# A softmax-routed expert kernel on one core: tokens laid out by unit pairs, stores with rows of 8 KB, and new order lists

## The chip, the core and the metric

The kernel runs on 1 of the 8 cores of one Trainium2 chip, as one program. The metric is the device time of an execution, in microseconds (us). A core has five engines with a queue each: TensorE (PE, its weight loads shown apart as PEld), VectorE (DVE), ScalarE (ACT), GpSimd (POOL) and SyncE (SP, which here only issues DMAs). Sixteen DMA engines move the data of all queues.

## The reference

Two layers follow each other. The first is a gated recurrence over the time axis, for 4 sequences of 5056 tokens with 256 channels; the second is a soft mixture of 8 experts with 4 slots each, over all 20224 tokens of the first one's output:

```python
# recurrence: per channel, along the tokens of a sequence
sig_r, sig_i = sigmoid(r_gate), sigmoid(i_gate)
a_t = exp(8.0 * sig_r * log(clip(sigmoid(a_param), 1e-6, 1 - 1e-6)))
x_gated = sqrt(maximum(1 - a_t * a_t, 1e-6)) * sig_i * x
h = a_t[:, t] * h + x_gated[:, t];  y[:, t] = h
# soft mixture: X is y as (20224, 256)
logits = X @ phi                                 # (20224, 32)
d = softmax of logits over all tokens            # per slot
slot_input = d.T @ X                             # (32, 256)
slot_out[e] = relu(slot_input[e] @ w1[e]) @ w2[e]   # w1 (256, 1024), w2 (1024, 256)
c = softmax of logits over the 32 slots          # per token
out = c @ slot_out                               # (20224, 256)
```

The sum over all tokens in `d.T @ X` splits the kernel: nothing can be stored before the last token has been scanned and the experts have run.

## The kernel before, in words

Tokens are cut into 40 blocks (quads) of QT = 512, the last of 256. UNITS puts them together: block 0 alone, then pairs (1,2), (3,4) to (37,38), and block 39 alone: 21 units. Every piece of work is a task of a planner, named by kind and number, and the lists ORDER write out for each engine in which order the tasks stand in its queue. An engine takes them strictly in that order. The durations that are given to the tasks were used to find an order; with ORDER set they only decide where warm-up transposes go and which buffer a task gets.

The tasks that matter here, by name:

- D (SP) loads r, i or x of a block: partition p holds 4 tokens that follow each other, so a row of 4 KB. SP's queue ends with the stores OD.
- TR, SR: PE transposes r, ACT takes tanh of it. The result goes to A, which holds channels on partitions and the unit's tokens in time order along the row. SI is the gate of i, EX the exponential (ACT), SQ the square (POOL), RT the square root (ACT), U the product of gate and x (POOL), TU its transposes (PE), ST and SC the scaling and the scan (DVE), which leaves h in A.
- TY (PE, L958) transposes h back to tokens on partitions, four transposes for 256 tokens, and YC copies it from PSUM to the buffer yn, on DVE or ACT.
- Blocks form groups of softmax, g = 0 to 10. LG (PE, L1009) gives the logits of up to 4 blocks at once, 32 partitions for each block. LE (DVE, L1022) keeps them and takes the running maximum M; LD subtracts it (POOL, and DVE for the last two groups), TE transposes, ES takes exp (ACT), AC (PE, L1083) multiplies with yn, AE adds it into accS with the correction DM (ACT).
- For the softmax over slots of each group: CT (PE, L1438) transposes the logits, CM and CS subtract the maximum (DVE), CE takes exp (ACT, L1455), RR sums (DVE, L1459), CN scales (POOL), CH and CL split the result in a high and a low part (DVE, POOL).
- The seam: after the last scan SC20.1 come LE9, LE10, the merging of the strips' maxima (MT, MX, MR, MC, WJ, WE, W), AC9, AC10, AE10, SP and SL (the slot inputs), then L1 and L2 for the 8 experts (PE, L1331 and L1379) with HS, HT, HR between them, SO, RS, SH and BD.
- The output: HP transposes the split weights of 8 x 128 tokens, HE copies them, OT (PE, L1526, two matmuls) makes 256 tokens of output, OE copies that from PSUM (ACT L1538, DVE L1540), and OD (SP, L1550) stores a block of 512 tokens from one buffer.

Before the change A is read in time order. LG takes 512 columns that follow each other, TY 128; CT reads every 4th column, and thereby its rows come out as the store needs them, 4 tokens on each partition.

Of the kernel before, what the change touches and what calls it, by code (L numbers as in the profile page):

```python
# [76 lines left out]
SIGR = False  # L77
CG = 3
ORDER = {
    "PE": """  # L80
# [8 lines left out]
        LG7.1 TY30.0 TU18.0 TY30.2 TY31.0 TY31.2 TE7 TU18.1 TY33.0 TY33.2 AC7.0 AC7.1 AC7.2 AC7.3 TU19.0 TY34.0 TY32.2 LG8.0 LG8.1 TY34.2 TY35.0
        TY36.0 TU19.1 TY36.2 TE8 TY35.2 LG9.0 AC8.0 AC8.1 TU20.0 TU20.1 LG9.1 AC8.2 AC8.3 LG10.0 LG10.1 TY37.0 TY37.2 TY39.0 MT TY38.0 TE9 TY38.2 TE10  # L90
        MC AC9.0 AC9.1 AC9.2 AC9.3 AC10.0 AC10.1 SP DN L1.0 L1.1 L1.2 L1.3 L1.4 HT0 L1.5 L1.6 L2.0 L2.1 L1.7 L2.2 HT1 L2.3 L2.4 L2.5 L2.6 L2.7 HP0.8
        HP0.0 RS HP2.0 CT3 HP1.8 HP1.0 OT0.6 OT0.4 OT0.2 OT0.0 OT0.12 OT0.8 OT1.0 OT1.2 OT0.10 OT0.14 OT1.6 OT1.4 CT6 HP2.8 CT4 OT2.2 OT2.0 OT2.6
# [11 lines left out]
        YC29.2 RT18.0 YC30.0 YC30.2 YC31.0 DM7 ES7 RT19.0 YC33.0 YC33.2 EX20.0 YC34.0 YC32.2 SI39 CE0 YC34.2 EX20.1 YC36.0 YC35.0 YC36.2 ES8 YC35.2
        RT20.0 CE1 YC37.2 DM8 CE2 YC37.0 YC38.0 ES9 YC39.0 ES10 DM10 WE YC38.2 DM9 HE0.0 BD01 BD00 OE0.4 HE1.0 OE0.2 CE3 OE1.2 OE0.10 HE1.8 HE2.0
        OE0.14 OE1.4 OE1.6 OE2.0 OE2.2 HE2.8 CE4 OE2.12 OE2.14 OE2.8 OE1.12 HE3.8 OE2.10 CE6 OE1.10 HE3.0 OE3.8 CE5 OE3.10 OE3.12 OE3.2 HE4.0 OE3.14
        OE3.4 OE3.6 OE4.0 OE4.8 CE7 OE4.12 OE4.6 HE5.8 HE5.0 OE4.10 OE5.6 OE5.8 OE5.10 OE5.2 CE8 OE5.12 HE6.8 OE5.14 OE6.12 OE6.4 OE6.6 CE9 OE6.8
# [9 lines left out]
        YC25.2 ST14.1 ST14.0 SC14.1 SC14.0 ST15.1 YC24.2 SC15.1 ST15.0 AE5 LE6 SC15.0 YC26.0 ST16.0 SC16.0 ST16.1 YC27.2 YC28.0 SC16.1 YC28.2 ST17.0
        AE6 SC17.0 ST17.1 LE7 SC17.1 ST18.0 YC31.2 SC18.0 ST18.1 AE7 SC18.1 ST19.0 LE8 SC19.0 ST19.1 SC19.1 ST20.0 ST20.1 SC20.0 SC20.1 LE9 RR0 LE10
        LD9 LD10 MX MR WJ AE8 AE9 W AE10 CH0 SL RD HS0 HR0 RR1 HS1 HR1 CH1 RR2 CH2 SO HE0.8 SH BD11 BD10 CM3 CS3 OE0.6 OE0.0 OE0.8 OE1.0 RR3 OE0.12
        CM6 CS6 CM4 CS4 OE2.4 CH3 OE2.6 RR4 OE1.14 OE1.8 CH4 CM5 CS5 CM7 RR6 OE3.0 RR5 HE4.8 CS7 CH5 OE4.4 OE4.2 RR7 CH6 OE4.14 CM8 OE5.4 CH7 CS8  # L120
# [1468 lines left out]
```

## Time and profile before

| what | us |
|---|---|
| median of 3 runs | 300.62 (299.88 to 300.74) |
| the profiled execution | 300.04 |
| its span, from the first to the last instruction | 298.3 |
| busy PE / DVE / ACT / POOL | 259.9 / 232.3 / 251.2 / 204.5 |
| moved by DMA | 100.02 MB (78.94 MB read, 20.71 MB written) |
| mean granted TensorE clock | 0.988 |

Times inside the trace count from the span's start. In rows of the time line the columns are the start, the duration of all instructions that the row merges, the engine, the line, the operation, what it writes and reads, and how many; a bracket tells the idle time before and who ended it. A line number is one of the kernel before, and several tasks of a kind share one line.

### The profile page before, as it was taken

What the parts mean: (1) busy time and instruction counts of PE and PEld (TensorE: products, weight loads), DVE (VectorE), ACT (ScalarE), POOL (GpSimd) and SP (SyncE); (2) the same over time, 40 slices, a digit from 0 to 9 for tenths busy, and PEclk for the clock granted to TensorE, in tenths of its full rate; (3) what the DMA queues carried; (4) which work ended last, traced back from release to release, by engine and by line L of the source; (5) the groups of instructions that cost most, each with busy time, mean ns of one, the idle gap of its engine ahead of it and who ended that gap; (6) DMA issues with size and microseconds to landing.
All of it is one profiled execution on the core that took longest, in us unless ns stands there. A gap on an engine that the chain in (4) does not pass through costs nothing.

```text
span 298.3 us, 5854 instructions
## 1 busy us (share of the span) xinstructions
PE 259.9 (87%) x2223; PEld 198.9 (67%) x2223; DVE 232.3 (78%) x289; ACT 251.2 (84%) x271; POOL 204.5 (69%) x150
## 2 busy tenths in 40 slices
PE   6998698899897997969978888999989999999990
PEld 6997697577564864747656556566556588888760
DVE  0047849898979999899999999999962489896820
ACT  5899999999999999997999999999650058978680
POOL 4297999778999798997499998983431513372310
PEclk9999999999999999979999999999999999999997
DMA  6999999997875999794996499599999029999997
GB/s 229 414 409 409 402 408 410 407 408 281 322 291 208 396 415 407 274 401 116 396 392 264 174 335 365 229 385 362 358 405 351 6 78 398 404 402 404 402 409 288
DMA packets 30287, 100.02 MB, mean 335 GB/s; under 512 B 3378, under 2 KB 3380, under 8 KB 30260
## 3 DMA queue, kind: packets, MB, share of 16 engines
q1 hardware_dynamic: 30256, 99.66, 86.6%
q8 instruction: 17, 0.28, 0.4%
q14 instruction: 10, 0.08, 0.1%
q10 hardware_dynamic: 4, 0.00, 0.0%
HBM read 78.94 MB, written 20.71 MB: 334 GB/s over the span
## 4 chain that ended last, share of the span: by engine, by line
PE 35%; ACT 24%; DVE 14%; DMA 11%; POOL 6%; issue 6%; SPq 0%; ACTq 0%; POOLq 0%; DVEq 0%
DVE b L934 7%; PE bank L1526 7%; DMA b<-in_i_gate_dram 6%; PE pair L788 5%; ACT b L881 4%; DVE pair L917 4%; PE pair L900 4%; POOL b L834 4%; ACT b L812 3%; DMA st<-in_moe_w_dram 3%; ACT b L799 3%; ACT b L866 3%; PE one L1526 3%; ACT L881 3%; POOL b L850 2%
## 5 line engine op out<-in xcount | busy, mean ns | idle before, releaser
L850 POOL TENSOR_TENSOR b<-b 128x1024 f32<-128x1024 f32 (+2 forms) x41 | 73.6, 1816 | 9.0 <-ACT b L866 4.7
L834 POOL TENSOR_TENSOR b<-b,b 128x1024 f32<-128x1024 f32 x32 | 75.4, 2379 | 6.0 <-ACT b L814 4.3
L917 DVE SCALAR_TENSOR_TENSOR pair<-b,pair 128x1024 f32<-128x1024 f32 (+2 forms) x42 | 47.9, 1154 | 11.9 <-ACT b L881 8.1
L900 PE MATMUL pair<-ident,b 128*128 128x128 f32 x380 | 49.4, 278 | 7.3 <-DVE b L934 3.0
L900 PEld LDWEIGHTS pair<-ident,b 128*128 128x128 f32 x380 | 42.3, 143 | 15.7 <-POOL b L834 4.7
L934 DVE TENSOR_TENSOR_SCAN b<-b,pair 128x1024 f32<-128x1024 f32 (+6 forms) x26 | 47.6, 1848 | 0.2
L788 PE MATMUL pair<-ident,st 128*128 128x128 f32 x316 | 42.1, 280 | 5.2 <-DVE b L934 2.1
L934 DVE TENSOR_TENSOR_SCAN b<-b,b,pair 128x1024 f32<-128x1024 f32 (+2 forms) x22 | 45.4, 2073 | 0.4
L788 PEld LDWEIGHTS pair<-ident,st 128*128 128x128 f32 x316 | 35.4, 143 | 12.8 <-ACT b L799 4.9
L799 ACT ACTIVATE b<-pair 128x1024 f32<-128x1024 f32 (+1 forms) x40 | 39.4, 1012 | 4.6 <-PE pair L788 4.4
L866 ACT ACTIVATE b<-b,ca 128x2048 f32<-128x2048 f32 (+3 forms) x24 | 42.7, 1795 | 0.2
L958 PE MATMUL one<-ident,b 128*128 128x128 f32 x208 | 31.6, 281 | 7.2 <-DVE yn L974 2.5
L958 PEld LDWEIGHTS one<-ident,b 128*128 128x128 f32 x208 | 22.6, 141 | 17.3 <-DVE yn L974 6.6
L1526 PE MATMUL bank<-bd,hT 128*128 128x512 f32 x118 | 31.7, 400 | 0.3 <-DVE hT L1516 0.3
L1469 POOL TENSOR_TENSOR b<-b,rs_all 128x512 f32<-128x512 f32 (+2 forms) x11 | 10.6, 960 | 29.8 <-DVE rs_all L1461 23.2
L881 ACT ACTIVATE b<-b 128x2048 f32<-128x2048 f32 (+2 forms) x17 | 29.8, 1785 | 0.1
L1514 ACT CAST hT<-bank 128x512 fp32r<-128x512 f32 x14 | 8.3, 600 | 21.4 <-PE bank L1503 20.6
L812 ACT ACTIVATE b<-b 128x2048 f32<-128x2048 f32 x14 | 26.0, 1906 | 0.1
L1526 PEld LDWEIGHTS bank<-bd,hT 128*128 128x128 f32 x118 | 21.3, 188 | 5.4 <-ACT st L1538 0.8
L1538 ACT COPY st<-bank 128x512 f32<-128x512 f32 x33 | 18.8, 603 | 6.9 <-PE bank L1526 4.5
L974 DVE COPY yn<-one 128x512 f32<-128x512 f32 x32 | 21.2, 682 | 2.2 <-PE one L958 2.1
L1009 PE MATMUL one<-b,phi_sb 128*32 128x512 f32 x152 | 21.3, 618 | 0.0
(146 smaller groups left out, 438.4 us busy)
## 6 DMA issues: line engine op xcount, KB each, us to landing
b<-in_x_dram SPq DMA_DIRECT2D x39, 512.0 KB, 7.4
st<-in_r_gate_dram SPq DMA_DIRECT2D x38, 512.0 KB, 8.1
b<-in_i_gate_dram SPq DMA_DIRECT2D x38, 512.0 KB, 8.4
b<-in_moe_w_dram SPq DMA_DIRECT2D x28, 512.0 KB, 6.2
out_dram<-st SPq DMA_DIRECT2D x28, 512.0 KB, 4.4
out_dram<-b SPq DMA_DIRECT2D x10, 512.0 KB, 4.6
st<-in_moe_w_dram SPq DMA_DIRECT2D x4, 512.0 KB, 8.0
st<-in_r_gate_dram SPq DMA_DIRECT2D x3, 256.0 KB, 2.9
```

The source lines that it names most:

```text
L788: nc.tensor.transpose(out=o[:, m, :], in_=raw("r", q)[:, m * D + h * P : m * D + (h + 1) * P], identity=ident,)
L799: nc.scalar.activation(dst, t(rp)[:, :, :c], AF.Sigmoid if SIGR else AF.Tanh, scale=1.0 if SIGR else 0.5)
L812: nc.scalar.activation(v, v, AF.Sigmoid)
L834: eng.tensor_tensor(out=o, in0=a, in1=b, op=ALU.mult)
L850: eng.tensor_tensor(out=t(Nb[p])[:, h, :c], in0=v, in1=v, op=ALU.mult)
L866: nc.scalar.activation(v, v, AF.Exp, scale=ca[:, h : h + 1], bias=ca[:, h : h + 1])
L881: nc.scalar.activation(v, v, AF.Sqrt, bias=quarter if f != 1.0 else f, scale=-f)
L900: nc.tensor.matmul(o[:, m, :], raw(nm, q)[:, m * D + h * P : m * D + (h + 1) * P], ident, is_transpose=True, start=(nm == nms[0] and m == ...
L917: nc.vector.scalar_tensor_tensor(v, t(Nb[p])[:, h, :c], 0.5e-3 if gate_of(quads(p)[0]) == "E" else 1e-3, v, op0=ALU.max, op1=ALU.mult)
L934: nc.vector.tensor_tensor_scan(dst, dst, flat()[:, s0:s1], init, op0=ALU.mult, op1=ALU.add)
L958: nc.tensor.transpose(out=flat()[:, b * D + h * P : b * D + (h + 1) * P], in_=t(A[p])[:, h, o : o + P], identity=ident,)
L1526: nc.tensor.matmul(t(op), t(hT)[:, b * P // 2 : (b + 2) * P // 2], T["bd"][part].rearrange("p i d -> p (i d)"), start=(part == 0), stop=(p ...
```

## The change

The unit, not the block, now decides which token lies where on the way back to token order. In a pair of 1024 tokens, partition c takes tokens 8c to 8c + 7. So column m of the transposed h is every 8th column of A (every 4th in block 0, every 2nd in block 39), and `tokens` gives that view to TY and LG. From there on, the two blocks of a pair are the lower and the upper four columns m, not its first and second 512 tokens. CT then reads columns that follow each other. The output of a pair lies in one buffer of 2048 floats per partition, and one store writes it with rows of 8 KB. The first group keeps separate stores of half rows for blocks 1 and 2.

Groups follow the units: 3 blocks, nine times 4 blocks (two units each), and the last one of 256 tokens as two strips of 128. Before there were nine groups of 4, one of 2, and one of three half blocks. As group 0 fills only 96 partitions, M and accS are preset for the rest. LD of the last two groups may go to DVE or POOL (it is on DVE still). The loads of r, i, x and the weights are the same, in another order. There are 22 stores where there were 41, and 41 AC where there were 42.

The core of the diff (of ORDER, all of whose lists change, one place; of the planner's durations, which change by a few hundredths of a microsecond, two):

```diff
     "DVE": """
-        ... SC20.0 SC20.1 LE9 RR0 LE10
-        LD9 LD10 MX MR WJ AE8 AE9 W AE10 CH0 SL RD HS0 HR0 RR1 ...
+        ... SC20.0 SC20.1 LE9 LE10 AE8 LD9 LD10 YC38.2 MX MR
+        WJ W AE9 AE10 SL RR1 RR2 RR0 RD HS0 CH1 HR0 ...
...
-            lat = {"PE": 0.25, "ACT": 0.13, "DVE": 0.13, "POOL": 0.12, "SP": 2.6}[eng[0]]
+            lat = {"PE": PEL, "ACT": 0.13, "DVE": 0.13, "POOL": 0.12, "SP": 2.6}[eng[0]]
...
-    groups = [[(q, 0, QT) for q in range(g, g + J)] for g in range(0, NQ - J, J)]
-    rest = list(range(len(groups) * J, NQ))
-    groups.append([(q, 0, QT) for q in rest[:2]])
-    half = QT // 2
-    tail = []
-    for q in rest[2:]:
-        tail += [(q, o, half) for o in range(0, qlen(q), half)]
-    assert len(rest) == J and len(tail) <= J and all(qlen(q) % half == 0 for q in rest)
-    groups.append(tail)
+    groups = [[(q, 0, QT) for q in range(J - 1)]]
+    groups += [[(q, 0, QT) for q in range(g, g + J)] for g in range(J - 1, NQ - 1, J)]
+    groups.append([(NQ - 1, o, P) for o in range(0, qlen(NQ - 1), P)])
     NGR = len(groups)
+    assert sorted({q for sg in groups for q, _, _ in sg}) == list(range(NQ)) and qlen(NQ - 1) == 2 * P
+
+    def tokens(q, b0=0, nb=J):
+
+        p, i = unit[q]
+
+        def view(h):
+            v = t(A[p])[:, h, : plen(p)].rearrange("q (c m) -> q m c", c=P)
+            k = i * J + b0
+            return v[:, k, :] if nb == 1 else v[:, k : k + nb, :]
+
+        return view
     if tc is not None:
         M = sb.tile([P, NGR], F32, name="M")
         dm = sb.tile([P, NGR], F32, name="dm")
...
+        first = NS * len(groups[0])
+        nc.gpsimd.memset(M[first:, 0:1], NEG)
+        nc.gpsimd.memset(accS[first:], 0.0)
 
     t_const = add("POOL", "const", 2.1, prio=-100, emit=e_const)
...
                 for b in range(nb):
-                    o = i * QT + (b0 + b) * P
                     for h in range(H):
                         nc.tensor.transpose(
                             out=flat()[:, b * D + h * P : b * D + (h + 1) * P],
-                            in_=t(A[p])[:, h, o : o + P],
+                            in_=tokens(q, b0 + b, 1)(h),
                             identity=ident,
                         )
 
...
                 for j, (q, o, _) in enumerate(segs):
-                    o += unit[q][1] * QT
                     nc.tensor.matmul(
                         t(lp)[32 * j : 32 * j + NS, :L], phi_sb[:, h, :],
-                        t(A[unit[q][0]])[:, h, o : o + L], start=(h == 0), stop=(h == H - 1),
+                        tokens(q, o // P, L // P)(h), start=(h == 0), stop=(h == H - 1),
                     )
 
-            lg = add("PE", f"LG{g}.{h}", L * 0.00195,
+            lg = add("PE", f"LG{g}.{h}", L * 0.0019,
                      deps=[SC[(p, h2)] for p in ps_ for h2 in range(h + 1)] + [ld[("x", PHI)]], gate=begun(lg),
                      prio=pos - LGP + fin, emit=e_lg, alloc=[] if h else [lp],
...
-        deng = LDENG if g < NGR - 2 else "D"
+        both = g >= NGR - 2
+        deng = {}
 
...
         def e_ae():
             if g == 0:
-                nc.vector.tensor_copy(out=accS, in_=t(acc)[:, : D + 1])
+                nc.vector.tensor_copy(out=accS[:rows], in_=t(acc)[:rows, : D + 1])
             else:
                 nc.vector.scalar_tensor_tensor(
...
-            v = lS(g)[:rows, :L].rearrange("q (p n) -> q n p", n=nb)
+            v = lS(g)[:rows, :L].rearrange("q (n p) -> q n p", n=nb)
...
-        ogs = [Buf(("st", "b", "yn"), f"og{g}.{j}") for j in range(n)]
-        for og in ogs:
-            og.late = ("begun", l1s[-1])
+        wide = {}
+        ogs = []
+        for j, (q, o, _) in enumerate(segs):
+            p, i_ = unit[q]
+            if len(quads(p)) == 2 and i_ or o:
+                ogs.append(ogs[-1])
+            else:
+                ogs.append(Buf("b" if len(quads(p)) == 2 else ("st", "yn", "b"), f"og{g}.{j}"))
+                ogs[-1].late = ("begun", l1s[-1])
+            wide[j] = (unit[q][1] * J if o == 0 else 1) * D if len(quads(p)) == 2 or o else 0
...
-                def e_oe(b0=b0, op=op, og=ogs[j]):
-                    dst = t(og)[:, b0 * D : (b0 + 2) * D]
+                def e_oe(b0=b0, op=op, og=ogs[j], w=wide[j]):
+                    dst = t(og)[:, w + b0 * D : w + (b0 + 2) * D]
...
+        js = []
         for j, (q, o, _) in enumerate(segs):
-
-            def e_od(q=q, o=o, L=L, nb=nb, og=ogs[j]):
-                a0 = q * QT + o
-                nc.sync.dma_start(
-                    out=out[a0 : a0 + L, :].rearrange("(p n) d -> p (n d)", n=nb), in_=t(og)[:, : nb * D])
-
-            add("SP", f"OD{g}.{j}", 1.30 * nb / J, deps=done[j], prio=100 + 8 * i + 4 + j, emit=e_od, uses=[ogs[j]], kind="out")
+            if o:
+                continue
+            two = len(quads(unit[q][0])) == 2
+            if two and g > 0 and unit[q][1]:
+                continue
+            def e_od(q=q, og=ogs[j], g=g):
+                p, i = unit[q]
+                t0 = UNITS[p][0] * QT
+                v = out[t0 : t0 + plen(p), :].rearrange("(m n) d -> m (n d)", n=plen(p) // P)
+                s = t(og)[:, : plen(p) // P * D]
+                if g == 0 and len(quads(p)) == 2:
+                    v, s = v[:, i * J * D : (i + 1) * J * D], s[:, i * J * D : (i + 1) * J * D]
+                nc.sync.dma_start(out=v, in_=s)
+            of = [j] if g == 0 else [j, j + 1] if two or L < QT else [j]
+            add("SP", f"OD{g}.{j}", 1.28 * (2 * P if L < QT else QT * len(of)) / QT, deps=[x for a in of for x in done.get(a, [])],
+                prio=100 + 8 * i + 4 + j, emit=e_od, uses=[ogs[j]], kind="out")
```

How the lists move the instructions is shown at three places. Numbers behind a name are buffers. DVE from the two last scans of block 39 (L934), before:

```order
L934 SCALAR_TENSOR_TENSOR b_66<-b_66,b_69,pair_92 128x256
L934 SCALAR_TENSOR_TENSOR b_66<-b_66,b_69,pair_93 128x256
L1021 COPY M<-M 32x1 x2
L1022 TENSOR_SCALAR b_73,M<-one_86,M 64x512
L1459 TENSOR_REDUCE rs_all<-b_66 128x16
L1460 TENSOR_SCALAR rs_all<-rs_all 128x16
L1461 RECIPROCAL rs_all<-rs_all 128x16
L1021 COPY M<-M 32x1
L1022 TENSOR_SCALAR b_73,M<-bank_2111,M 96x256
L1042 TENSOR_SCALAR lD_83<-one_86,M 64x512
L1042 TENSOR_SCALAR lD_82<-bank_2111,M 96x256
```

After (L947 is the scan, L1033 is LE, L1114 AE, L1058 LD, L986 YC):

```order
L947 SCALAR_TENSOR_TENSOR b_74<-b_74,b_68,pair_92 128x256
L947 SCALAR_TENSOR_TENSOR b_74<-b_74,b_68,pair_93 128x256
L1033 TENSOR_SCALAR b_66,M<-one_86,M 128x512
L1032 COPY M<-M 32x1 x2
L1033 TENSOR_SCALAR b_66,M<-bank_2096,M 64x128
L1114 SCALAR_TENSOR_TENSOR accS<-accS,dm,one_87 128x257
L1058 TENSOR_SCALAR lD_83<-one_86,M 128x512
L1058 TENSOR_SCALAR lD_82<-bank_2096,M 64x128
L986 COPY yn_76<-bank_2098 128x2x256
L1283 TENSOR_REDUCE mmax<-bank_2101 1x32
L1285 COPY mrep<-mmax 1x128
```

The sums of group 0 (L1459 to L1461) have left the place between the two maxima; AE8 and a copy YC38.2 have come in behind them.

PE at the first output matmuls (OT, two rows each; hT is the transposed weight buffer that HE fills, bd the expert outputs), before:

```order
L1526 MATMUL bank_2112<-bd_2203,hT_2206 128x512
L1526 MATMUL bank_2112<-bd_2204,hT_2206 128x512
L1526 MATMUL bank_2116<-bd_2203,hT_2206 128x512
L1526 MATMUL bank_2116<-bd_2204,hT_2206 128x512
L1526 MATMUL one_86<-bd_2203,hT_2206 128x512
L1526 MATMUL one_86<-bd_2204,hT_2206 128x512
L1526 MATMUL bank_2111<-bd_2203,hT_2205 128x512
L1526 MATMUL bank_2111<-bd_2204,hT_2205 128x512
```

After:

```order
L1549 MATMUL bank_2096<-bd_2185,hT_2188 128x512
L1549 MATMUL bank_2096<-bd_2186,hT_2188 128x512
L1549 MATMUL bank_2101<-bd_2185,hT_2187 128x512
L1549 MATMUL bank_2101<-bd_2186,hT_2187 128x512
L1549 MATMUL bank_2099<-bd_2185,hT_2187 128x512
L1549 MATMUL bank_2099<-bd_2186,hT_2187 128x512
L1549 MATMUL bank_2098<-bd_2185,hT_2188 128x512
L1549 MATMUL bank_2098<-bd_2186,hT_2188 128x512
L1549 MATMUL bank_2100<-bd_2185,hT_2188 128x512
L1549 MATMUL bank_2100<-bd_2186,hT_2188 128x512
```

Before, OT0.6 and OT0.4, which fill block 1, stand first. Now OT0.6, OT0.8, OT0.10 and OT0.4 follow each other, and the second half of block 1 is the fourth.

SP where the last weight loads end and the stores begin, before:

```order
L1236 DMA b_69<-in_moe_w_dram 128x1024 x2
L1238 DMA b_67<-in_moe_w_dram 128x2x512 x4
L1550 DMA out_dram<-st_64 128x1024
L1550 DMA out_dram<-st_63 128x1024
L1550 DMA out_dram<-st_65 128x1024
L1550 DMA out_dram<-st_62 128x1024
L1550 DMA out_dram<-b_66 128x1024
L1550 DMA out_dram<-st_64 128x1024
```

After:

```order
L1253 DMA b_66<-in_moe_w_dram 128x2x512 x2
L1585 DMA out_dram<-b_69 128x1024
L1585 DMA out_dram<-st_64 128x1024
L1585 DMA out_dram<-b_69 128x1024
L1585 DMA out_dram<-b_75 128x2048
L1585 DMA out_dram<-b_66 128x2048
L1585 DMA out_dram<-b_73 128x2048 x2
L1585 DMA out_dram<-b_75 128x2048
```

The stores of 128 x 1024 floats become 128 x 2048 after the first three.

More of the change, by code (lines that the diff above doesn't have):

```diff
@@ L77 @@
 SIGR = False
+SIWITH = {}
 CG = 3
@@ L89 @@
[L89 to L92, printed above, removed]
@@ new lines @@
+        TY33.0 TY35.0 TY33.2 TE8 TY36.2 TY35.2 AC8.0 AC8.1 LG9.0 TU20.0 TU20.1 AC8.2 LG9.1 AC8.3 LG10.0 LG10.1 TY38.0 TY38.2 TY37.0 TY37.2 MT TE9
+        TY39.0 TE10 MC AC9.0 AC9.1 AC9.2 AC9.3 AC10.0 SP DN L1.0 L1.1 L1.2 L1.3 L1.4 HT0 L1.5 L1.6 L1.7 L2.0 CT3 HT1 L2.1 L2.2 L2.3 L2.4 L2.5 L2.6
+        L2.7 HP0.8 HP0.0 RS CT6 HP1.0 HP2.0 OT0.6 OT0.8 OT0.10 OT0.4 OT0.0 OT0.2 OT1.2 OT1.0 OT1.4 OT1.6 OT2.4 OT2.2 OT2.0 OT2.6 CT5 CT4 HP1.8 HP3.0
+        HP2.8 HP3.8 OT1.8 OT1.14 OT1.12 OT1.10 OT2.12 OT2.8 OT2.10 OT3.10 OT2.14 OT3.12 OT3.8 OT3.14 OT3.0 OT3.4 CT7 HP4.8 HP4.0 CT10 OT3.2 OT3.6
@@ L104 @@
[L104 to L107, printed above, removed]
@@ new lines @@
+        RT12.0 RT11.0 YC18.0 YC17.0 RT13.0 YC18.2 SR27 SR28 SR29 YC17.2 DM4 SR30 SR31 EX14.0 SR33 EX14.1 SR32 SR34 ES4 EX16.0 EX16.1 DM5 ES5 SI27 SI29
+        RT14.0 RT17.0 RT15.0 SI31 SI33 SR35 SR37 RT16.0 YC23.2 YC25.0 SR36 SR38 YC25.2 EX18.0 YC27.0 ES6 EX18.1 DM6 SI35 YC28.0 SR39 SI37 RT18.0
+        YC29.0 YC31.2 YC29.2 YC30.0 DM7 ES7 YC30.2 RT19.0 YC32.2 EX20.0 SI39 YC34.0 EX20.1 YC36.0 YC34.2 YC33.0 YC35.0 YC33.2 ES8 YC36.2 RT20.0 DM8
+        YC35.2 YC38.0 DM9 YC37.0 YC37.2 ES9 ES10 YC39.0 WE CE1 DM10 CE2 CE0 HS1 CE3 HE0.0 BD00 BD01 OE0.6 OE0.0 OE0.10 HE2.0 OE0.8 CE6 OE1.6 OE1.2
@@ L117 @@
[L117 to L120, printed above, removed]
@@ new lines @@
+        YC11.2 YC12.2 YC15.0 YC16.0 YC13.2 SC9.1 YC15.2 CM2 AE3 CS2 YC16.2 ST10.0 ST10.1 SC10.0 SC10.1 ST11.0 SC11.0 LE4 ST11.1 SC11.1 ST12.0 SC12.0
+        ST12.1 SC12.1 ST13.0 LE5 SC13.0 ST13.1 AE4 SC13.1 YC23.0 YC22.0 YC20.0 YC21.0 YC19.0 YC19.2 YC21.2 YC20.2 YC22.2 ST14.0 ST14.1 SC14.0 SC14.1
+        ST15.0 AE5 SC15.0 ST15.1 YC24.0 SC15.1 LE6 YC24.2 ST16.0 YC26.0 SC16.0 ST17.0 YC26.2 SC17.0 ST16.1 LE7 SC16.1 AE6 YC27.2 YC31.0 ST17.1 YC28.2
+        SC17.1 ST18.0 YC32.0 ST18.1 SC18.0 SC18.1 AE7 ST19.0 LE8 ST19.1 SC19.0 SC19.1 ST20.0 ST20.1 SC20.0 SC20.1 LE9 LE10 AE8 LD9 LD10 YC38.2 MX MR
@@ L173 @@
 class Buf:
[L176 removed]
+    __slots__ = ("tags", "tag", "slot", "users", "name", "need", "late", "mate", "kept", "led")
     def __init__(self, tags, name=""):
@@ L436, in tag_for @@
     def tag_for(self, b, taken={}):
+        if b.led and b.kept is None:
+            return None
         for g in b.tags:
@@ L1019, in e_le @@
         def e_le():
-            for r0 in range(rows, P, 32):
+            for r0 in range(rows, P, 32) if g else ():
                 nc.vector.tensor_copy(out=M[r0 : r0 + 32, g : g + 1], in_=M[r0 : r0 + 32, g - 1 : g])
@@ L1275, in merge_tasks @@
             out=small["wj"], in0=mm, in1=t(mp)[:, P : P + 1], op=ALU.subtract))
-        a = add("ACT", "WE", 0.2, deps=[a], prio=-60, kind="exp",
+        a = add("ACT", "WE", 0.1, deps=[a], prio=-60, kind="exp",
                 emit=lambda: nc.scalar.activation(small["wj"], small["wj"], AF.Exp))
@@ L1453, in mk_c @@
                     out=cn(), in0=v3(t(cp)), in1=t(rm)[:, :m, :].broadcast_to([P, m, NS]), op=ALU.subtract))
-        e = add("ACT", f"CE{g}", 0.12 + 0.43 * nb * rows / QT, deps=[k], prio=pr, kind="exp", gate=("gates_done",),
+        e = add("ACT", f"CE{g}", 0.1 + 0.43 * nb * rows / QT, deps=[k], prio=pr, kind="exp", gate=("gates_done",),
                 uses=[lSb[g // 4]], emit=lambda: nc.scalar.activation(lS(g)[:, : m * NS], lS(g)[:, : m * NS], AF.Exp))
```

128 lines of the change are left out of this document (66 added, 62 removed).

## The prediction

> **What bounds the kernel now.** I read the busy tenths first, then the sums over stretches, then what ScalarE (ACT) waited for, and last the seam between the two halves and the output, instruction by instruction. The page first, cut to ACT, the DMA engines and what they moved in 40 slices of 7.5 us:
>
> ```profile
> ACT  5899999999999999997999999999650058978680
> ...
> DMA  6999999997875999794996499599999029999997
> GB/s 229 414 409 409 402 408 410 407 408 281 322 291 208 396 415 407 274 401 116 396 392 264 174 335 365 229 385 362 358 405 351 6 78 398 404 402 404 402 409 288
> ```
>
> ACT is full until slice 28 and the DMA engines from slice 34 on; in slice 32 neither does anything. The sums (PE, PEld, DVE, ACT, POOL busy, the clock, DMA share, GB/s) and ACT's waits after 15 us (in total, times, longest):
>
> ```profile
> 15.00:212.00 197.00, 172.24 (x1524) 130.43 (x1524) 178.11 (x167) 193.72 (x166) 172.22 (x92) 0.99 0.89 342
> 227.00:230.00 3.00, 3.00 (x54) 1.74 (x49) 1.74 (x5) 0.00 (x0) 0.00 (x0) 1.00 1.04 380
> 246.00:292.00 46.00, 43.45 (x227) 35.13 (x225) 33.14 (x71) 37.20 (x73) 16.35 (x16) 1.00 1.01 403
> ...
> ACT b L799 <- PE pair L788: 2.2, 3, 1.5
> ```
>
> From 15 to 212 us ACT idles 197.00 - 193.72 = 3.3 us, so before the seam an order can win only what it takes off ACT and some of those 3.3 us. PE has 24.8 us of idle there. From 246 us the stores run at 403 GB/s with a DMA share above 1, and PE beside them is 94% busy: a co-bound.
>
> The seam, on VectorE (DVE) and then PE, from the end of the last scan:
>
> ```profile
> 213.99 0.31 DVE L1021 COPY M<-M 32x1 f32<-32x1 f32 x2
> 214.31 0.74 DVE L1022 TENSOR_SCALAR_CACHE_REDUCE b<-one,M 64x512 f32<-64x512 f32 x1
> ...
> 214.99 0.67 DVE L1459 TENSOR_REDUCE rs_all<-b 128x16 f32<-128x512 f32 x1
> ...
> 216.19 0.15 DVE L1021 COPY M<-M 32x1 f32<-32x1 f32 x1
> 216.37 0.48 DVE L1022 TENSOR_SCALAR_CACHE_REDUCE b<-bank,M 96x256 f32<-96x256 f32 x1
> ...
> 216.78 0.74 DVE L1042 TENSOR_SCALAR lD<-one,M 64x512 f32<-64x512 f32 x1
> ...
> 219.21 0.48 DVE L1099 SCALAR_TENSOR_TENSOR accS<-accS,dm,one 128x257 f32<-128x257 f32 x1
> ...
> 217.58 0.46 PE L1053 MATMUL one<-ident,lD 64*128 64x64 f32 x4
> ...
> 219.03 2.80 PE L1083 MATMUL bank<-yn,eS 128*32 128x257 f32 x28
> 222.43 0.63 PE L1284 MATMUL one<-W,accS 128*128 128x32 f32 x4 [0.60 <-DVE accS L1099]
> ```
>
> A reader should see one chain: the two maxima LE9 and LE10 (L1022) with the row sums RR0 (L1459) between them, the difference LD9, its transposes, the accumulation AC9 and AC10 (28 records), and SP (L1284) at 222.43, which opens the expert layers. Every microsecond here moves the end.
>
> **The change, step by step.** (1) *ACT up to the last root.* The order lists put 152 ACT steps before; 150 now: CE0 goes behind the seam, and one copy YC goes to DVE, whose count of copies ahead of the last scan stays 47. Their sizes, from neighbours of the same kind:
>
> ```profile
> 216.95 0.62 ACT L1455 ACTIVATE b<-b 128x512 f32<-128x512 f32 x1
> 217.47 1.06 ACT L972 COPY yn<-bank 128x512 f32<-128x512 f32 x2
> 218.42 0.40 ACT L1063 ACTIVATE eS<-one 128x256 f32<-128x256 f32 x1
> ...
> 208.82 0.64 ACT L1063 ACTIVATE eS<-one 128x512 f32<-128x512 f32 x1
> ```
>
> One CE occupies 217.47 - 216.95 = 0.52 us and one copy 1.06 / 2 = 0.5: **-1.0 us**. Table loads stay 26. The rest of the rearrangement makes or removes waits: at best -3.3, and at worst I bound it by the same amount upward, since the order before left that much. I take 0.
>
> (2) *The seam.* New durations from the rows above. LE9 has 128 rows and no copies of M, 0.68; LE10 takes two copies (0.30) and 128 columns, for which I scale 0.74 for 512 and 0.48 for 256 to 0.35; AE8 has been put ahead of LD9, 0.43 (its matmuls stand on PE ahead of LG10, so it doesn't wait). LD9 thus begins 1.76 us after the scan, before 216.78 - 213.99 = 2.79. From LD9 to the first AC were 219.03 - 216.78 = 2.25; ES9 over 512 columns instead of 256 adds 0.24. AC falls from six rounds of 4 to five: 2.80 x 5/6 = 2.33. From AC's end (221.83) to SP were 0.60. Sum 1.76 + 2.49 + 2.33 + 0.60 = 7.2 against 222.43 - 213.99 = 8.4: **-1.2 us**. The four TY ahead of MT on PE end about where LD9 does, so YC38.2 and ES9 are late next; bounds -1.7 and -0.7. RR0 to RR2 move behind SL, beside L1 on PE, at 216.19 - 214.99 = 1.2 each, 3.6 together, about what the first four L1 take on PE before HS0 is due: 0, and +0.5 if HS0 comes later. CT3 stood behind RS and moves into the L2 run; PE does the same work: 0.
>
> (3) *The first stores.* What stands there before: CT, HP and the first output matmuls OT on PE, the first store on SP, the last OT, the last stores, and how long a single store of 256 KB takes to land.
>
> ```profile
> 240.52 0.65 PE L1438 MATMUL bank<-ident,b 128*128 128x128 f32 x4
> 241.00 1.04 PE L1503 MATMUL bank<-ident,st 128*128 128x128 f32 x8
> 241.80 0.71 PE L1526 MATMUL one<-bd,hT 128*128 128x512 f32 x2
> 242.34 1.07 PE L1526 MATMUL bank<-bd,hT 128*128 128x512 f32 x4
> 242.84 0.68 DVE L1540 COPY st<-one 128x512 f32<-128x512 f32 x1
> ...
> 243.26 0.62 PE L1526 MATMUL one<-bd,hT 128*128 128x512 f32 x2
> ...
> 243.61 3.72 SPq L1550 DMA_DIRECT2D out_dram<-st  x4
> ...
> 288.58 2.09 PE L1526 MATMUL bank<-bd,hT 128*128 128x512 f32 x8 [0.35 <-DVE hT L1516]
> ...
> 291.84 2.45 SPq L1550 DMA_DIRECT2D out_dram<-st  x3
> ...
> out_dram<-b SPq DMA_DIRECT2D x1, 256.0 KB, 3.2
> ```
>
> Before, two OT fill the first block, and its store goes 243.61 - 241.80 = 1.81 us after the first OT. Now the block is full with the fourth OT; at (243.26 - 242.34) / 2 = 0.46 each and a copy of 0.7 its store goes after 2.6: **+0.8 us**; bounds 0 and +1.0. From then on blocks of 1 MB come as fast as they are stored.
>
> (4) *The stores themselves.* 41 stores of 4 KB rows (the last ones 2 KB) become 22, most with 8 KB rows. No row shows 8 KB. The nearest are 2 KB rows (the last w2 loads, 227 to 230 us) at 380 GB/s and 4 KB rows at 403: per DMA engine 2048 / 23.75 = 86.2 ns and 4096 / 25.2 = 162.6 ns. So 76.4 ns carry 2 KB and some 10 ns are paid per row; 8 KB would take 162.6 + 2 x 76.4 = 315 ns, or 416 GB/s. 20.7 MB then take 49.8 us instead of 51.4: **-1.6 us**. Bounds: 0, if a row is cut to pieces of 4 KB, and -3.1, if nothing is paid per row (2048 bytes in 76.4 ns are 429 GB/s). I take -1.6, since rows of 2 and 4 KB do differ. "DMA: Bandwidth & Descriptors" of the Trainium skill (Bandwidth) asks for transfers of 1 MiB and more, and gives 435 GB/s as the ceiling of the fabric; the trace has 403 with half that size, and by the ceiling the term would be an estimated -3.8 us.
>
> PE caps this: the last OT ends at 290.67, 48.9 us after the first, and the last block of 1 MB can only be sent after it. From there one copy and wait (1.0), 1.3 MB at 416 GB/s (3.1) and landing (2.5: 3.2 less 0.65 for 256 KB) give 55.5 us after the first OT; the DMA count gives 2.6 + (298.3 - 243.61) - 1.6 = 55.7, against 298.3 - 241.80 = 56.5 before. Both agree, so (3) and (4) hold together at -0.8.
>
> (5) *Strided reads.* TY now loads every 8th column of A as weights, LG streams every 8th column as moving data; CT loses a stride of 4. Rows: loads for CT (stride 4) and TY (contiguous), and the matmuls of LG and TY.
>
> ```profile
> L1438 PEld LDWEIGHTS bank<-ident,b 128*128 128x128 f32 (+2 forms) x26 | 3.8, 207 | 0.3 <-DVE st L1540 0.2
> L958 PEld LDWEIGHTS one<-ident,b 128*128 128x128 f32 x208 | 22.6, 141 | 17.3 <-DVE yn L974 6.6 <-ACT yn L972 4.2 <-DVE b L934 1.8
> L1009 PE MATMUL one<-b,phi_sb 128*32 128x512 f32 x152 | 21.3, 618 | 0.0
> ```
>
> A strided load takes 66 ns longer, but it lies under the matmul before it: four CT advance in 241.00 - 240.52 = 0.48, 0.12 each, eight HP in 0.80, 0.10 each. On 316 transposes (8 for each of 39.5 blocks) 0.02 us are 6.3 us of PE, under its 24.8 us of idle: 0. For LG no strided row exists. At 66 ns per 128 columns a pass over 512 pays 0.26 us; 10 groups x 2 halves x 2 passes make +10.6 us of PE at worst, none at best; I take none, because CT's pace hardly moved. "Advanced Engine Details and Errata" of the Trainium skill (SBUF Cachelines) speaks against it: lines are 16 bytes, and an access that goes to a new line each time pays; by it LG would pay too, which is the slower rival below. A stride of 4 floats goes to a new line each time already, and the trace shows that as 66 ns that are hidden.
>
> (6) *Loads.* Five weight loads now stand ahead of the last x block on SP's queue, two before.
>
> ```profile
> 183.89 1.83 SPq L735 DMA_DIRECT2D b<-in_x_dram  x2
> 190.11 3.48 SPq L1238 DMA_DIRECT2D b<-in_moe_w_dram  x4
> ...
> 208.02 1.28 POOL L834 TENSOR_TENSOR b<-st,b 128x512 f32<-128x512 f32 x1
> ```
>
> Three weights are 3 MB, 7.8 us at 403 GB/s; the block, issued at 185 us, is used by U39 at 208: covered, 0. If the queue stalls for free buffers longer than those 23 us, everything behind it slips.
>
> **Sum.** -1.0 - 1.2 + 0.8 - 1.6 = -3.0 us on the profiled execution's 300.04 (its span of 298.3 and 1.7 around it): 297.0. That execution lies 0.6 below the median of 300.62, so against the median I forecast 297.6.
>
> **Rivals.** *The rows bring nothing*: (4) is 0 and the end falls by (1) to (3) alone, -1.4: 299.2. For it: the stores already show a share above 1. Against: the 2 KB rows. *The order also drops ACT's waits*: 2.5 of the 3.3 us more, 295.1. For it, three of those waits are for one kind of step, TR on PE; against, PE is nearer its limit with every strided load. *Slower, by LG alone*: if four strips that stream at once, each with a stride, pay the 0.26 us per pass, PE gets 10.6 us, nearly all of it ahead of the seam; half of that reaching ACT through late TR (SR waits for TR already, 2.2 us) gives +5.3: 302.9. It decides from +3.9 us on. *New waits* in an order that no trace has run, at the bound of (1), +3.3: 300.9, no change.
>
> **How the numbers follow.** Forecast 0.40 (296.3 to 298.8), rows bring nothing 0.20, waits dropped 0.12, LG slow 0.14, new waits 0.14. A change under 0.3%, 0.9 us, can't be told from none here. Faster: 0.39 + 0.15 + 0.11 = 0.65. Same: 0.05 of the second and 0.10 of the last: 0.15. Slower 0.20, from LG and the rest. The range runs from 294.7, the case of dropped waits, to 301.9, which leaves out most of the LG case.
>
> **What would show it.** Right: ACT's last root about 1 us earlier; RR0 gone from between LE9 and LE10, and SP some 7.2 us after the last scan; the first store 2.6 us after the first OT; stores at about 416 GB/s from then on; the LG group still near 618 ns. Wrong: LG well above 618 ns; stores still at 403; new idle on ACT behind PE or SP; or DMA gaps in the output while a block of 1 MB is being filled.

## The result, and the profile after

The changed kernel takes 307.41 us (median of 4 runs, 307.11 to 308.78) where the kernel before takes 300.53 (4 runs, 299.88 to 300.74): a ratio of 1.0241, interval 1.0207 to 1.0276. It is slower by 2.4%; 297.6 was forecast. The profiled execution took 307.37 us with a span of 305.6, so 7.3 us more span than before. The ratios here and below are of fast executions alone: three of the later kernels have one execution each, more than 1.5% above their own fastest, that the ratio leaves out.

The page of the changed kernel first: ACT, the DMA engines and their GB/s in 40 slices, here of 7.6 us.

```profile
ACT  5899999999999999999989989898760149868750
DMA  7999999998896898849977796499999109999997
GB/s 249 415 409 410 401 408 381 367 413 346 290 394 229 315 408 304 326 130 339 409 260 262 289 335 252 157 377 392 324 351 372 63 0 409 385 406 391 418 417 291
```

ACT, at nine in all slices but one from the third to the 28th before, has eights in slices 21, 24, 26 and 28: something makes it wait while the recurrence still runs. The output, from slice 34, swings between 385 and 418 GB/s where it stood at 398 to 409. The sums over the stretch that the prediction used show the same (columns as there):

```profile
15.00:212.00 197.00, 181.00 (x1447) 128.31 (x1446) 171.59 (x162) 187.96 (x155) 170.18 (x102) 1.00 0.88 330
```

ACT idles 9.0 us instead of 3.3, and PE only 16.0 instead of 24.8: PE has more to do, and ACT seems to pay for it. The groups of instructions of the changed kernel say with what:

```profile
L1020 PE MATMUL one<-b,phi_sb 128*32 128x512 f32 x156 | 39.9, 1092 | 0.3 <-DVE yn L986 0.3
...
L970 PEld LDWEIGHTS one<-ident,b 128*128 128x128 f32 x172 | 22.2, 193 | 12.3 <-DVE yn L986 4.2 <-DVE accS L1114 2.7 <-issue 2.7
```

L1020 is LG. Four strips stream at once, so 156 passes of 1092 ns keep PE busy for 39.9 us; before, 152 passes took 21.3. One pass of one line, minimum, median and maximum in ns, before and then after:

```profile
L1009 PE MATMUL one<-b,phi_sb x152: 592/592/1063, 53.2 to 212.1; 128*32 128x512 f32 x152
```

```profile
L1020 PE MATMUL one<-b,phi_sb x156: 1077/1097/1127, 37.8 to 220.2; 128*32 128x512 f32 x156
```

By the medians a strided pass costs 505 ns more than a contiguous one. The loads of TY (L970) went from 141 to 193 ns, 52 ns more where 66 were foreseen. What waited for PE in the changed kernel, ACT from 15 to 217 us and then DVE from 45 to 217 us (in total, times, longest):

```profile
ACT b L812 <- PE pair L801: 2.4, 6, 0.6
ACT yn L984 <- PE pair L970: 1.6, 2, 1.1
ACT eS L1078 <- PE one L1068: 1.5, 2, 0.8
```

```profile
DVE pair L930 <- PE pair L913: 4.5, 7, 1.5
DVE b L1033 <- PE one L1020: 3.3, 3, 1.8
```

And DVE before, from 45 to 212 us, where L917 is ST:

```profile
DVE pair L917 <- PE pair L900: 2.5, 5, 1.0
```

SR still waits for TR (2.4 us, 2.2 before), and ST (L930) for TU, longer than before. New are YC for TY, ES for TE, and on DVE LE (L1033) for LG itself. That fits a PE on which each LG lasts longer, so that what stands behind it in the queue comes late; the first experiment tests it. The time line of the changed kernel at the seam and at the output:

```profile
219.45 1.38 DVE L947 TENSOR_TENSOR_SCAN b<-b,b,pair 128x256 f32<-128x256 f32 x2
221.38 0.75 DVE L1033 TENSOR_SCALAR_CACHE_REDUCE b<-one,M 128x512 f32<-128x512 f32 x1 [0.55 <-PE one L1020]
...
228.81 0.63 PE L1299 MATMUL bank<-W,accS 128*128 128x32 f32 x4 [0.80 <-DVE accS L1114]
...
248.32 2.60 PE L1549 MATMUL bank<-bd,hT 128*128 128x512 f32 x10
...
251.38 0.36 SPq L1585 DMA_DIRECT2D out_dram<-b  x1
...
296.92 0.62 PE L1549 MATMUL bank<-bd,hT 128*128 128x512 f32 x2
...
299.35 0.41 SPq L1585 DMA_DIRECT2D out_dram<-st  x1
```

The span cut at these rows gives the whole difference; the last column is the repaired kernel of the second experiment:

| stretch, us | before | after | forecast | repaired |
|---|---|---|---|---|
| start to the end of the last scan | 213.96 | 220.83 | -1.0 | 212.07 |
| from there to SP | 8.47 | 7.98 | -1.2 | 7.47 |
| SP to the first OT | 19.37 | 19.51 | 0 | 19.59 |
| first OT to the first store | 1.81 | 3.06 | +0.8 | 3.05 |
| first store to the end | 54.69 | 54.22 | -1.6 | 54.32 |

6.9 - 0.5 + 0.1 + 1.25 - 0.5 = +7.3 us. One remark on the order shown before the prediction: before the change the two rows of OT0.6, at 241.80 us, stand just ahead of the first row of the fence of PE.

### The profile page after: what moved, and what is told of

The parts are those of the page before. It is cut to its first block, busy times and chain, and to the rows that moved or that the text cites. A ratio compares the mean times of both kernels' runs of the same rounds, so it can differ in the third digit from the quotient of the medians.

```text
span 305.6 us, 5781 instructions
## 1 busy us (share of the span) xinstructions
PE 274.6 (90%) x2211; PEld 198.5 (65%) x2211; DVE 236.5 (77%) x292; ACT 250.2 (82%) x267; POOL 205.7 (67%) x153
## 4 chain that ended last, share of the span: by engine, by line
PE 50%; ACT 22%; DVE 12%; POOL 6%; issue 6%; DMA 2%; SPq 0%; DVEq 0%; ACTq 0%; POOLq 0%
PE bank L1549 9%; PE one L1020 9%; ACT b L812 6%; PE pair L913 6%; DVE b L947 5%; ACT b L879 4%; PE pair L801 4%; ACT b L894 3%; POOL b L863 3%; DVE pair L930 3%; PE one L1549 3%; PE pair L970 3%; PE bank L1394 2%; PE one L970 2%; PE one L1098 2%
## 5 line engine op out<-in xcount | busy, mean ns | idle before, releaser
L847 POOL TENSOR_TENSOR b<-b,b 128x1024 f32<-128x1024 f32 x36 | 84.8, 2379 | 6.4 <-DMA b<-in_i_gate_dram 2.5
L863 POOL TENSOR_TENSOR b<-b 128x1024 f32<-128x1024 f32 (+2 forms) x42 | 74.5, 1792 | 18.6 <-ACT b L879 11.5
L930 DVE SCALAR_TENSOR_TENSOR pair<-b,pair 128x1024 f32<-128x1024 f32 (+2 forms) x42 | 48.0, 1156 | 12.9 <-PE pair L913 9.0
L913 PEld LDWEIGHTS pair<-ident,b 128*128 128x128 f32 x380 | 41.6, 141 | 16.3 <-issue 8.0
L947 DVE TENSOR_TENSOR_SCAN b<-b,pair 128x1024 f32<-128x1024 f32 (+6 forms) x26 | 47.5, 1846 | 0.2
L947 DVE TENSOR_TENSOR_SCAN b<-b,b,pair 128x1024 f32<-128x1024 f32 (+2 forms) x22 | 45.3, 2073 | 0.4
L1020 PE MATMUL one<-b,phi_sb 128*32 128x512 f32 x156 | 39.9, 1092 | 0.3 <-DVE yn L986 0.3
L1549 PE MATMUL bank<-bd,hT 128*128 128x512 f32 x122 | 33.0, 399 | 0.4 <-ACT hT L1537 0.2
L970 PE MATMUL one<-ident,b 128*128 128x128 f32 x172 | 27.6, 289 | 6.0 <-DVE yn L986 2.7
L970 PEld LDWEIGHTS one<-ident,b 128*128 128x128 f32 x172 | 22.2, 193 | 12.3 <-DVE yn L986 4.2
L1561 ACT COPY b<-bank 128x512 f32<-128x512 f32 x39 | 22.6, 599 | 8.6 <-PE bank L1549 8.6
L1549 PEld LDWEIGHTS bank<-bd,hT 128*128 128x128 f32 x122 | 22.1, 188 | 5.6 <-ACT hT L1537 0.9
L986 DVE COPY yn<-one 128x512 f32<-128x512 f32 x29 | 19.2, 683 | 7.2 <-PE one L970 7.1
L970 PEld LDWEIGHTS pair<-ident,b 128*128 128x128 f32 x124 | 16.3, 194 | 10.1 <-issue 2.6
```

The source lines that it names most:

```text
L847: eng.tensor_tensor(out=o, in0=a, in1=b, op=ALU.mult)
L863: eng.tensor_tensor(out=t(Nb[p])[:, h, :c], in0=v, in1=v, op=ALU.mult)
L913: nc.tensor.matmul(o[:, m, :], raw(nm, q)[:, m * D + h * P : m * D + (h + 1) * P], ident, is_transpose=True, start=(nm == nms[0] and m == ...
L930: nc.vector.scalar_tensor_tensor(v, t(Nb[p])[:, h, :c], 0.5e-3 if gate_of(quads(p)[0]) == "E" else 1e-3, v, op0=ALU.max, op1=ALU.mult)
L947: nc.vector.tensor_tensor_scan(dst, dst, flat()[:, s0:s1], init, op0=ALU.mult, op1=ALU.add)
L970: nc.tensor.transpose(out=flat()[:, b * D + h * P : b * D + (h + 1) * P], in_=tokens(q, b0 + b, 1)(h), identity=ident,)
```

## The experiments

**LG alone, taken out and put in.** If the strided stream of LG is the cause, the changed kernel with a contiguous LG must come back, and the kernel before must get slow with a strided one. In both kernels the logits belong to other tokens, so only their time counts.

```diff
-    tokens(q, o // P, L // P)(h), start=(h == 0), ...
+    t(A[unit[q][0]])[:, h, unit[q][1] * QT + o : unit[q][1] * QT + o + L], start=(h == 0), ...
```

> The changed kernel, but LG streams 512 columns of A that follow each other, so its logits belong to other tokens than TY's; all else is as changed. Theory LG (the strided stream doubles a pass, 592 to 1097 ns, and PE makes everything ahead of the last scan late): a pass back at 592 ns, the last scan ends about 7 us earlier, time about 300.5 us. Theory order (the new lists wait by themselves): a pass at 592 ns, but the time stays above 305 us. Theory TY (strided weight loads): above 304 us.

300.2 us (10 runs, 298.51 to 302.0), ratio to before 0.999 (0.9959 to 1.0021). LG's passes take 600 ns on average, 20.6 us in all. The stretch from 15 to 212 us:

```profile
15.00:212.00 197.00, 174.69 (x1502) 134.52 (x1504) 177.41 (x168) 192.79 (x165) 174.04 (x108) 0.98 0.90 342
```

PE is busy 6.3 us less there than in the changed kernel although it gets further (1502 instructions instead of 1447), and ACT idles 4.2 us instead of 9.0. Seven microseconds, the whole loss, hang on this one operand. The other way round, the kernel before with the view `tokens` in LG:

```diff
-    t(A[unit[q][0]])[:, h, o : o + L], start=(h == 0), ...
+    tokens(q, o // P, L // P)(h), start=(h == 0), ...
```

> The kernel before with one edit: LG streams every 8th column of a pair (every 4th of block 0), as in the changed kernel, so its logits belong to other tokens. Order, groups, TY and stores are those before. Theory LG: a pass at some 1097 ns, PE some 18 us busier, time 305 to 308 us. Theory order: under 302 us.

311.87 us (4 runs, 311.54 to 312.65), ratio 1.0365 (1.0321 to 1.0408). LG took 40.1 us at 1094 ns a pass, and in

```profile
15.00:212.00 197.00, 177.12 (x1452) 125.51 (x1453) 170.18 (x160) 185.93 (x151) 168.24 (x86) 0.99 0.85 328
```

ACT idles 11.1 us. On DVE, LE now waits for LG, which it didn't before:

```profile
DVE b L1032 <- PE one L1019: 7.5, 7, 1.7
```

The stride costs the old order some 11 us and the new one some 7. So under the stride the rest of the change is worth some 4 us, and without it next to nothing; what in the new order takes the stride better wasn't separated further.

**The same result without the stride.** The logits don't need to stand in the order of the column m: LG may take runs of 4 neighbouring columns, 8 apart, in the order of the partitions, if TE and CT then pick the columns apart.

```diff
+            if runs and nb > 1:
+                return t(A[p])[:, h, : plen(p)].rearrange("q (c m) -> q c m", c=P)[:, :, k : k + nb]
...
-    out=t(ep)[:, b * rows : (b + 1) * rows], in_=t(lD)[:rows, b * P : (b + 1) * P],
+    out=t(ep)[:, b * rows : (b + 1) * rows],
+    in_=t(lD)[:rows, :L].rearrange("q (p n) -> q n p", n=nb)[:, b, :],
...
-    v = lS(g)[:rows, :L].rearrange("q (n p) -> q n p", n=nb)
+    v = lS(g)[:rows, :L].rearrange("q (p n) -> q n p", n=nb)
```

> The changed kernel with the same tokens in LG, streamed in another order of columns: runs of 4 floats that follow each other, 8 apart, and TE and CT take every 4th column instead. It computes the same. If the price of LG is one line of memory per column (theory LG in the form that four columns of a line are served together), a pass is near 592 ns and the time near that of the first run, 300.5 us. If any break in the stream costs, a pass stays near 1097 ns and the time near 307 us.

300.5 us (10 runs, 298.17 to 302.39), ratio 0.9984 (0.9945 to 1.0022). Repeated on another chip it gave 300.54, ratio 0.9993 (0.9959 to 1.0028). Its group of LG, and its time line at the places of the table:

```profile
L1022 PE MATMUL one<-b,phi_sb 128*32 128x512 f32 x156 | 20.6, 600 | 0.3 <-DVE yn L988 0.3
```

```profile
210.69 1.38 DVE L949 TENSOR_TENSOR_SCAN b<-b,b,pair 128x256 f32<-128x256 f32 x2
...
219.54 0.63 PE L1302 MATMUL bank<-W,accS 128*128 128x32 f32 x4 [0.80 <-DVE accS L1117]
...
239.13 2.57 PE L1552 MATMUL bank<-bd,hT 128*128 128x512 f32 x10
...
242.18 0.36 SPq L1588 DMA_DIRECT2D out_dram<-b  x1
```

A pass over runs of 4 costs what a contiguous one does, 600 ns on average, and no loss from the strided loads that TE and CT now have can be seen (300.5 us against 300.2 in the first experiment, with intervals that overlap). This execution (298.25 us, span 296.5) is 1.8 us shorter than that of before; the median is not. The last section says what lies between them.

**TY contiguous as well.**

```diff
-    in_=tokens(q, b0 + b, 1)(h),
+    in_=t(A[p])[:, h, i * QT + (b0 + b) * P : i * QT + (b0 + b + 1) * P],
```

> As the run before, and TY also loads columns that follow each other (its output then belongs to other tokens). Theory LG: within 0.7 us of the run before. Theory TY: 3 us or more below it, with weight loads of TY back from 193 to 141 ns. Theory order: no difference either, but both above 305 us.

299.66 us (10 runs, 297.52 to 302.42), ratio 0.9952 (0.9912 to 0.9993), against 0.999 of the first experiment on the same chip. TY's loads fell from 194 to 146 ns. From 15 to 212 us PE is busy 173.55 us instead of 174.69, and ACT idles 3.1 us instead of 4.2. The medians differ by 0.5 us and the ratios by 0.4%, or 1.1 us, with intervals that overlap. So the strided loads are hidden for the most part: the 3 us that would have spoken for TY are out, a cost of up to about 1 us isn't.

**Which stride pays, and who.** One kernel with another pattern in each group: stride 8 in group 1 (L1024), 4 in group 2 (L1026), 2 in group 3 (L1028), stride 8 in one strip of four in group 4 (L1030, its neighbours L1032), runs of 4 in group 5 (L1034), runs of 2, 4 apart, in group 6 (L1036), stride 8 in two strips of group 8 (L1038), the rest contiguous (L1042). It ran once, in 299.93 us.

> The changed kernel with a different stream in LG for each softmax group, to price the stream itself (its logits belong to other tokens): group 1 every 8th column, 2 every 4th, 3 every 2nd, 4 every 8th in one strip of four and flat in the other three, 5 runs of 4 columns 8 apart, 6 runs of 2 columns 4 apart, 8 every 8th in two strips of four, all others flat. Theory line (each strip pays by itself whenever the next column lies in another 16 bytes): groups 1 and 2 at 1097 ns a pass, 3, 5 and 6 at 592, and in 4 and 8 the strided strips alone at 1097. Rival, a shared limit of the four strips: in groups 4 and 8 the price falls with the number of strided strips, one alone near 600 to 700 ns, or the flat strips beside them slow down too.

```profile
L1024 PE MATMUL one<-b,phi_sb x16: 1081/1090/1097, 62.7 to 67.5; 128*32 128x512 f32 x16
L1026 PE MATMUL one<-b,phi_sb x16: 1077/1092/1112, 87.4 to 90.2; 128*32 128x512 f32 x16
L1028 PE MATMUL one<-b,phi_sb x16: 610/612/637, 107.3 to 108.7; 128*32 128x512 f32 x16
L1030 PE MATMUL one<-b,phi_sb x4: 1097/1097/1098, 126.3 to 133.0; 128*32 128x512 f32 x4
L1032 PE MATMUL one<-b,phi_sb x12: 592/604/617, 126.3 to 132.6; 128*32 128x512 f32 x12
L1034 PE MATMUL one<-b,phi_sb x16: 592/604/617, 142.2 to 146.2; 128*32 128x512 f32 x16
L1036 PE MATMUL one<-b,phi_sb x16: 609/612/637, 164.5 to 171.7; 128*32 128x512 f32 x16
L1038 PE MATMUL one<-b,phi_sb x8: 1090/1097/1106, 196.7 to 199.9; 128*32 128x512 f32 x8
L1042 PE MATMUL one<-b,phi_sb x44: 592/592/617, 37.8 to 213.0; 128*32 128x512 f32 x44
```

Strides 4 and 8 cost the same, so it isn't the distance. Stride 2 and runs of 2 cost 20 ns, runs of 4 next to nothing (12 ns). One strip with a stride pays 1097 ns by itself while its three neighbours stay at 604: a limit that the four strips share is out. But the group ends with its slowest strip: the four strided passes of group 4 keep PE busy for 4.0 us, as long as all 16 of group 1. The step lies between one and two floats from the same 16 bytes. That is the rule of "Advanced Engine Details and Errata" of the Trainium skill (SBUF Cachelines): lines of 16 bytes, and two hits on a line for full performance. These rows agree with it and add the price for moving data, 505 ns on 512 columns, almost 1 ns for each.

**What the 8 KB rows bring.** In the repaired kernel, each store of a pair split into two with rows of 4 KB:

```diff
-    nc.sync.dma_start(out=v, in_=s)
+    if s.shape[-1] == 2 * J * D:
+        nc.sync.dma_start(out=v[:, : J * D], in_=s[:, : J * D])
+        nc.sync.dma_start(out=v[:, J * D :], in_=s[:, J * D :])
+    else:
+        nc.sync.dma_start(out=v, in_=s)
```

> The base, but each store of a pair goes out as two with rows of 4 KB, both when the pair is complete. Theory rows (a cost per row makes 8 KB rows 3% faster): 1.0 to 1.6 us slower than the base, and a full stretch of stores at 403 GB/s instead of some 430. Rival (the output is bound by PE and by when blocks are complete): within 0.5 us of the base, though the full stretches are slower.

300.92 us (12 runs, 299.2 to 302.23), ratio to before 1.0001 (0.9978 to 1.0023); the repaired kernel stood at 0.9993 on that chip. From the first store to the end it takes 54.9 us, against 54.3. So PE was taken off the output, by leaving out the low part of the split weights in OT (`for part in range(1)`, one matmul instead of two), once with 8 KB rows and once with the edit above. Both leave the low part of the product out, so they serve for the time alone.

> The changed kernel with runs of 4 columns in LG, and OT multiplies only with the high part of the expert outputs (the low part is left out), which takes half of OT's PE time off the output, some 18 us. If PE bounds the output: from the first store to the end falls from 54.3 to about 51 us, and the time by 2 to 3.5 us. If the DMA engines bound it: no more than 0.5 us.

> The run before with rows of 4 KB (each store of a pair as two). Where the DMA engines bound the output, the cost per row must show: 1.0 to 1.6 us slower than the run before, at 403 GB/s against some 415 to 430. If rows of 8 KB bring nothing by themselves: the same time within 0.4 us.

299.61 us (297.81 to 301.53) with 8 KB and 300.49 (299.05 to 302.07) with 4 KB, 10 runs each; ratios 0.9952 (0.9918 to 0.9987) and 0.9985 (0.9948 to 1.0021). From the first store to the end the profiled executions take 299.7 - 246.20 = 53.5 and 299.8 - 244.80 = 55.0 us; they end together because the first of them reached its first store 1.4 us later. The stretch from 258 to 286 us of four kernels: repaired with 8 KB rows, repaired with 4 KB rows, one part with 8 KB, one part with 4 KB.

```profile
258.00:286.00 28.00, 26.64 (x136) 20.56 (x135) 22.36 (x45) 20.29 (x40) 9.25 (x10) 1.00 0.98 405
```

```profile
258.00:286.00 28.00, 27.00 (x142) 21.14 (x140) 22.58 (x46) 19.65 (x39) 11.20 (x11) 1.00 1.01 402
```

```profile
258.00:286.00 28.00, 22.05 (x110) 15.69 (x108) 25.07 (x50) 22.42 (x45) 11.14 (x11) 0.96 1.01 417
```

```profile
258.00:286.00 28.00, 20.81 (x98) 14.79 (x97) 23.88 (x47) 21.23 (x44) 10.33 (x11) 0.94 1.02 405
```

The last two numbers of a row are read together. With one part PE has room, the DMA share stays above 1 in both, and 8 KB rows carry 417 GB/s against 405. With both parts PE is busy 95% of the stretch, and the 8 KB rows end at 405 with a share of 0.98: the DMA engines then have gaps, and what the rows save goes into them. In the medians 8 KB rows bring 0.9 us with one part, under the 1.0 to 1.6 expected, and the two intervals overlap. And taking half of OT off PE shortened the stretch only from 54.3 to 53.5 us, not to the 51 expected: with PE out of the way the DMA engines bound it at 417 GB/s.

**The first store earlier.** In the repaired kernel's lists, the four OT of the first block stand first on PE, and their copies OE0.4 and OE0.2 ahead of HE1.0, CM6, CH3 and CS6 on DVE. On ACT, OE0.10 and HE2.0 change places.

```diff
-  PE: ... OT0.6 OT0.8 OT0.10 OT0.4 OT0.0 OT0.2 OT1.2 ...
+  PE: ... OT0.6 OT0.4 OT0.0 OT0.2 OT0.8 OT0.10 OT1.2 ...
-  DVE: ... BD11 CM6 CH3 CS6 HE1.0 OE0.4 OE0.2 OE1.0 ...
+  DVE: ... BD11 OE0.4 OE0.2 HE1.0 CM6 CH3 CS6 OE1.0 ...
```

> The base, but the two output matmuls of block 1, then those of block 0, stand first on PE, and DVE copies them ahead of CM6, CH3, CS6 and HE1. The first store goes some 1.5 us earlier. If the DMA engines bound the output: 0.8 to 1.5 us faster than the base. If PE bounds it: within 0.4 us, with the gap moved further back.

301.7 us (12 runs, 299.39 to 304.1), ratio 1.0027 (0.9999 to 1.0056). The first OT of its time line at 241.69 us, the first store at 243.67, so 1.98 us apart instead of 3.05. But the last OT ends 50.4 us after the first, against 49.3, and the end comes 300.1 - 241.69 = 58.4 us after the first OT, against 296.5 - 239.13 = 57.4. The end came later by as much as the last OT. Of these 1.1 us the edit itself made 0.8: HE1.0, now behind the two copies, lets PE wait before its seventh OT.

```profile
245.49 2.60 PE L1552 MATMUL bank<-bd,hT 128*128 128x512 f32 x10 [0.78 <-DVE hT L1542]
```

So the end follows PE here and not the first store; what an earlier first store would bring with PE not held up wasn't tested.

**Fewer warm-ups.** The repaired kernel's runs spread wider than those of before. One idea was that its 128 warm-up transposes bring the granted clock down: WARMT from 60 to 25 leaves 100.

> The changed kernel with runs of 4 columns in LG, and the warm-up transposes on idle PE end at 25 us instead of 60 us of the plan. If they bring on the stretches of lower granted clock that this kernel has more of than the one before: the mean clock rises from 0.977 to 0.985 or more and the time falls to 298 to 299.5 us. If not: clock and time as the base, 300.5 us, or slower where PE now begins its transposes late.

300.29 us (10 runs, 297.89 to 302.41), ratio 0.9968 (0.9929 to 1.0007), the granted clock 0.975 on average, against 0.977 over the 22 executions of the repaired kernel. The spread stayed; the idea isn't supported.

## Why the prediction was wrong

**The step that failed is (5), for LG.** It took 0 for a strided stream, because the strided loads of CT hardly changed CT's pace. That row shows weight loads, which can lie under the matmul before them. LG's strided operand is the moving one, and its pass is itself the matmul: the pass went from 592 to 1097 ns, and PE's busy time with it. The dearest case was taken from the same loads, 66 ns for 128 columns or 260 ns a pass; measured are 505. So PE got 18.6 us (39.9 - 21.3) instead of 0 or at most 10.6. Its idle took part of it; the last scan ends 6.9 us later than before, and 8.8 later than in the repaired kernel. The slower rival named this mechanism, this line and this way to ACT; its price was half of the true one and its chance 0.14. The text even had, beside the row, a rule by which LG would pay, and let a row of another kind of access overrule it.

**(1), ACT up to the last root, -1.0:** about right as the size of the work. Up to the end of the last root, at 209.83 us in the repaired kernel and 211.88 before, ACT works 203.1 us instead of 204.3. It also idles 0.9 us less, 0.55 of that in the first 15 us, which (1) put at nothing. So the last scan ends 1.9 us earlier. Single waits came and went: from 15 to 210 us SR waits 0.6 us for TR, 2.2 before, and three others of 0.4 to 0.6 us are new.

```profile
15.00:212.00 197.00, 174.72 (x1519) 134.59 (x1516) 179.37 (x171) 193.98 (x167) 173.61 (x108) 0.99 0.91 344
...
ACT b L814 <- PE pair L803: 0.6, 2, 0.3
```

With the strided LG none of it can be seen.

**(2), the seam, 7.2 us:** 7.47 in the repaired kernel. In the changed one 7.98, because LE9 waits 0.55 us for LG9, which (2) did not have.

**(3), the first stores, +0.8:** +1.25. Four OT were counted at 0.46 each, 1.84 us; in the repaired kernel the fourth ends 2.1 us after the first began, because the first lasts longer than that pace. Another 0.2 us pass until the copy starts: OE0.4 stands behind CM6, CH3, CS6 and HE1.0 in DVE's queue. The bound was +1.0, so this was outside it.

**(4), the rows of 8 KB, -1.6:** the price was right where the DMA engines are the bound (417 GB/s against 405, and 1.5 us less in the two profiled executions). The kernel collected 0.5. With (3) the output was to take 0.8 us less; from the first OT to the end it takes 57.3 us, against 56.5 before. The cap by PE was worked out too, with 6.6 us behind the last OT; there are 305.6 - 297.54 = 8.1, the last store alone being issued 1.8 us after that OT and the end coming 6.25 later. So the cap by PE is the number to use, and not the count of what the DMA engines can do; it was 1.8 us too low, 1.5 of them behind the last OT.

**(6), the loads:** 0, as it came. In the repaired kernel the last block of x is issued at 195.4 us, ten later than before, and U39 takes it at 206.8 without a wait. **The strided loads of TY, also in (5):** taken as 0, measured at 0.5 to 1.1 us, which the runs can't tell from 0.

Without the stride, the forecast of -3.0 would have met -1.8 in the profiled execution of the repaired kernel, and no difference in its median.

## What to carry to other kernels

Price a stride by the role of the operand: as weights it can hide under the matmul before (at most about 1 us for all of TY here), as moving data it lengthens the matmul itself (18.6 us for LG), and a price of the one says nothing of the other. A layout that is wanted for the stores needn't be paid in the stream: keep at least two, better four, floats together in what PE streams, and undo the order in transposes, whose loads were mostly hidden here. And where two resources are both near full, give a gain on one of them only what the other leaves.
